# Writing the order of a spectrum filter loop by hand: groups and blocks in a software pipeline, program order pinned on three engines

## The chip, the cores and the metric

The kernel runs on one core of a Trainium2 chip. The metric is the device time of one execution in microseconds (us), the median of the runs named.

The engines are called by their short names: PE is the matrix engine, PEld its weight loads, DVE the vector engine, ACT the scalar engine, POOL (or GpSimd) the general one, SP the sync engine, whose queue issues most transfers.

## The reference

It is the backward pass of a gated sum of two filters over a sequence of 2048 positions and 1024 channels in bf16, together with the forward result:

```
g   = sigmoid((x * gate_w).sum(-1))
a   = irfft2(rfft2(x) * W)              # filter over sequence and channels
b   = causal convolution of B_u with a kernel K made from 12 parameter arrays (FFT of length 4096) + B_u * Dskip
out = g * a + (1 - g) * b
# the outputs: out, and the gradients of 12 inputs for a given grad_out
```

The part at issue is the stage that applies K's spectrum to two signals at once (one of the forward and one of the backward pass). We call it the filter stage. It works through the 1024 channels in eight blocks of 128.

## The kernel before

For each block the filter stage does five things. "First" is a short transform of the input by PE, evacuated by ACT into `st`, which DVE transposes to `Si`. "Second" transforms again, for 17 frequencies in groups of four, four, four, four and one; ACT evacuates to `XG`. "Products" multiplies by the spectrum `kb` on DVE into `PY`. "Inverse" takes `PY` through PE and ACT to `Vt`, and "lags" correlates another part of `PY` on PE. After the five groups DVE transposes `Vt` to `Vr`, and "last" finishes the block in four pieces: PE matmuls, then five DVE instructions with loaded tiles `am`, `gm`, `gom`, and two stores.

```
def middle(bi, Si):
    for gi, (p0, nk_) in enumerate(GRP):                 # (0,4) (4,4) (8,4) (12,4) (16,1)
        # load kb; second: XG  (PE reads Si[:, :, f, :], two bf16 out of every 64)
        # products: m, n -> PY      (DVE)
        # inverse:  PY -> Vt        (PE, ACT)
        # more products: g1, g2 -> PY[..., 256:384]   (DVE)
        # lags: PY -> pq            (PE)
    turn(Vr, Vt)                                         # two DVE transposes, 4.4 us
    return Vr

def last(bi, Vr):
    for hq in range(H16 // HQ):                          # four pieces
        am, gm, gom = three tiles, two buffers each
        nc.sync.dma_start(out=am[:], in_=av3[:, hs, csl])
        nc.sync.dma_start(out=gm[:], in_=gxv3[:, hs, csl])
        nc.sync.dma_start(out=gom[:], in_=gov3[:, hs, csl])
        # 8 matmuls Vr -> py
        TT(out=t_[:], in0=py[:, :, 0, :], in1=omg2[...], op=ALU.mult)
        TT(out=gm[:], in0=py[:, :, 1, :], in1=gm[:], op=ALU.add)
        TT(out=am[:], in0=t_[:], in1=am[:], op=ALU.add)
        TT(out=t_[:], in0=gom[:], in1=am[:], op=ALU.mult)
        nc.vector.tensor_reduce(out=ggall[:, bi, hs], in_=t_[:], axis=AX.X, op=ALU.add)
        nc.sync.dma_start(out=o0v[:, hs, csl], in_=am[:])
        nc.sync.dma_start(out=gxv3[:, hs, csl], in_=gm[:])      # the scratch gm was loaded from

xgs = load_pair(0)
Si = fwd1(0, xgs)                                        # "first" and its transpose
for bi in range(DC):                                     # eight blocks
    Vr = middle(bi, Si)
    if bi + 1 < DC:
        if bi % 2 == 1:
            xgs = load_pair((bi + 1) // 2)
        Si = fwd1(bi + 1, xgs)
    last(bi, Vr)
```

A scheduler may move instructions of one engine against each other where their data allow it, so the order in the program is only where it starts from. After the filter stage comes "the tail", which turns lags into gradients of the parameters; it begins with loads of 1.57 and 1.05 MB of parameters, 1.38 MB of a table `ORJ`, and tiles `A2t`.

## Time and profile before

| | before |
|---|---|
| time, median of the 4 runs beside the changed kernel | 1990.86 us |
| filter stage (first `Si` transpose to the sum that follows the last piece) | 1043.7 to 1752.7 us |
| from `Vr` transpose to `Vr` transpose, seven blocks | 88.2 us mean, 85.3 or 92.1 each but the first |
| tail | 239 us |

First the window table of the kernel before over most of the stage: how long each engine was busy (instructions in brackets), the granted clock of PE as a share of full speed, the mean busy share of the DMA engines, GB/s.

```profile
core 0: us, PE busy (x) PEld busy (x) DVE busy (x) ACT busy (x) POOL busy (x), PEclk, DMA share, GB/s
1045.00:1661.00 616.00, 357.96 (x1832) 210.29 (x1833) 311.83 (x615) 178.27 (x191) 0.00 (x0) 0.74 0.25 50
```

No engine is full: PE 58%, DVE 51%, ACT 29%. The clock of 0.74 belongs to the same picture. The Trainium skill, "TensorE: Matmul & The Clock Gate", Part 1: The HAM clock gate, says that the default is half the clock and that only sustained work lifts it. One 256-column matmul with a contiguous input follows the other by 0.107 us inside busy stretches (granted clock 1.00 at 1105.5 us) and by about 0.213 us after idle ones (granted clock 0.50 at 1231 us, after 13.4 us of idling).

The list of waits of the stage in the kernel before says who waits for whom: engine and what it was to work on, what came last, total us, number of waits, longest.

```profile
DVE m L985 <- ACT XG L922: 231.6, 33, 8.5
PEld L1003 <- DVE PY L988: 134.8, 32, 4.8
DVE gm L1043 <- DMA gm<-gx_scr: 61.0, 7, 13.3
DVE am L1044 <- DMA am<-a_scr: 22.1, 8, 11.7
```

DVE waits for ACT's evacuation of the second stage, PE waits for DVE's products: each group is a chain handed from engine to engine. The last two lines are waits for loads at block ends, 83 us in all. The largest of the `am` waits, 11.7 us, stands at the stage's end. The DVE timeline of one block end in the kernel before shows them (start in us, length, engine, line, instruction, and in brackets the idle time before it with what ended it; `...` marks lines left out):

```profile
1282.79 4.50 DVE L939 STREAM_TRANSPOSE Vr<-Vt 128x2048 f32<-128x2048 f32 x2 [0.42 <-ACT Vt L922]
1291.10 0.69 DVE L1042 TENSOR_TENSOR t__10724<-f_10715,omg_101 128x512 bf16<-128x512 f32 x1 [3.81 <-PE f_10715 L1040]
1292.30 4.49 DVE L939 STREAM_TRANSPOSE Si<-st 128x2048 f32<-128x2048 f32 x2
...
1311.87 0.69 DVE L1043 TENSOR_TENSOR gm<-f_10761,gm 128x512 bf16<-128x512 f32 x1 [11.38 <-DMA gm<-gx_scr]
...
1316.08 0.68 DVE L985 TENSOR_TENSOR m<-XG,kb 128x1024 bf16<-128x1024 bf16 x1
```

From the transpose of `Vr` to the first product of the next block DVE needs 33.3 us, of which 11.4 and 1.3 us are waits for loads, 3.8 us a wait for PE. The rest is DVE's own work: two transposes and most of the four pieces of the last stage.

### The profile page before, as it was taken

What the parts mean: (1) busy time and instruction counts of PE and PEld (TensorE: products, weight loads), DVE (VectorE), ACT (ScalarE), POOL (GpSimd) and SP (SyncE); (2) the same over time, 40 slices, a digit from 0 to 9 for tenths busy, and PEclk for the clock granted to TensorE, in tenths of its full rate; (3) what the DMA queues carried; (4) which work ended last, traced back from release to release, by engine and by line L of the source; (5) the groups of instructions that cost most, each with busy time, mean ns of one, the idle gap of its engine ahead of it and who ended that gap; (6) DMA issues with size and microseconds to landing.
All of it is one profiled execution on the core that took longest, in us unless ns stands there. A gap on an engine that the chain in (4) does not pass through costs nothing.

```text
span 1992.0 us, 25908 instructions
## 1 busy us (share of the span) xinstructions
PE 1206.2 (61%) x10318; PEld 732.4 (37%) x10342; DVE 1223.7 (61%) x2033; ACT 787.2 (40%) x820; POOL 45.3 (2%) x158
## 2 busy tenths in 40 slices
PE   1787668761036495757626465746546565549995
PEld 1444344430013253434413242423323343237773
DVE  8545667529889777876244546445445545537886
ACT  4443234323376957674232222313232332135441
POOL 0000012100000000000010000000000000000000
PEclk9999989995555575757767777868677776757777
DMA  2322523223123223322060512240241202386661
GB/s 88 97 43 85 165 81 81 66 76 98 38 79 131 106 85 124 129 90 101 33 226 12 92 31 64 32 91 15 62 76 47 64 17 64 16 263 215 213 202 43
DMA packets 185887, 181.48 MB, mean 91 GB/s; under 512 B 114723, under 2 KB 148515, under 8 KB 182566
## 3 DMA queue, kind: packets, MB, share of 16 engines
q1 hardware_dynamic: 176806, 175.36, 30.2%
q10 hardware_dynamic: 7632, 3.41, 0.6%
q0 software_dynamic: 1328, 1.05, 0.4%
q8 instruction: 81, 1.33, 0.3%
q14 instruction: 40, 0.33, 0.1%
HBM read 101.29 MB, written 77.95 MB: 90 GB/s over the span
## 4 chain that ended last, share of the span: by engine, by line
PE 42%; DVE 25%; ACT 13%; DMA 12%; issue 6%; SPq 1%; ACTq 0%; POOL 0%; DVEq 0%; POOLq 0%
PE kx L770 5%; PE pq L1019 4%; PE pr L1113 4%; DMA gx_scr<-gm 3%; PE p2i L444 3%; ACT st L922 2%; PE pT L1099 2%; DVE m L985 2%; ACT XG L922 2%; DVE n L986 2%; DMA out_dram<-am 1%; DVE Ue L491 1%; DMA am<-a_scr 1%; ACT Tsb L1103 1%; PE trp L738 1%
## 5 line engine op out<-in xcount | busy, mean ns | idle before, releaser
L985 DVE TENSOR_TENSOR m<-XG,kb 128x1024 bf16<-128x1024 bf16 (+1 forms) x80 | 48.5, 607 | 231.6 <-ACT XG L922 231.6
L1103 ACT ACTIVATE Tsb<-pT 128x672 bf16<-128x672 f32 x128 | 87.3, 728 | 68.6 <-PE pT L1099 67.6
L1099 PE MATMUL pT<-GKq,A2t 32*128 32x42 bf16 x2048 | 84.3, 243 | 43.1 <-DMA A2t<-at_3847 32.7
L1110 DVE TENSOR_TENSOR pd<-Tsb,ORJt 128x5376 bf16<-128x5376 bf16 x32 | 93.8, 2950 | 24.0 <-PE pr L1113 20.6
L1003 PEld LDWEIGHTS <-IC 128*128 128x128 bf16 x120 | 13.1, 127 | 255.6 <-DVE PY L988 134.8
L1019 PE MATMUL pq<-TKT,PY 128*128 128x321 bf16 x544 | 96.5, 333 | 0.0
L1099 PEld LDWEIGHTS <-A2t 32*128 32x128 bf16 x2048 | 65.3, 110 | 66.6 <-issue 63.0
L1113 PE MATMUL pr<-pd,ident 128*128 128x256 bf16 x504 | 77.2, 319 | 4.5 <-DVE pd L1110 4.5
L1019 PEld LDWEIGHTS <-PY 128*128 128x128 bf16 x544 | 59.6, 112 | 32.7 <-DVE PY L1012 1.6
L444 PE MATMUL p2i<-T_131,Z 128*128 128x512 bf16 x224 | 59.1, 381 | 6.8 <-DVE Z L413 3.4
L1113 PEld LDWEIGHTS <-ident 128*128 128x128 bf16 x504 | 54.8, 113 | 22.1 <-issue 6.1
L748 PE MATMUL pK<-wOR,AT 128*32 128x21 bf16 x1024 | 29.7, 207 | 48.0 <-ACT AT L743 24.7
L770 PE MATMUL kx<-Kc,TK_4047 128*128 128x256 bf16 x136 | 41.5, 305 | 22.9 <-DVE spk L778 12.1
L453 DVE CAST UV<-p2i 128x512 bf16<-128x512 f32 x28 | 19.3, 690 | 56.4 <-ACT UV L455 44.7
L743 ACT ACTIVATE AT<-trp 128x1024 bf16<-128x1024 bf16 x32 | 32.6, 1019 | 50.6 <-PE trp L738 50.4
L778 DVE CAST spk<-kx 128x1024 bf16<-128x1024 f32 x16 | 19.6, 1224 | 53.2 <-PE kx L770 53.1
L748 PEld LDWEIGHTS <-AT 128*32 128x32 bf16 x2048 | 23.8, 110 | 77.0 <-ACT AT L743 34.6
L681 PE MATMUL ph<-zrow,Lz 8*128 8x512 bf16 x64 | 30.2, 562 | 29.9 <-ACT EA L682 27.1
L986 DVE TENSOR_TENSOR n<-XG,kb 128x1024 bf16<-128x1024 bf16 (+1 forms) x80 | 48.2, 603 | 0.0
L949 PEld LDWEIGHTS <-S1f 128*128 128x128 bf16 x256 | 25.5, 101 | 59.5 <-issue 53.9
L776 ACT ACTIVATE spk<-kx 128x1024 bf16<-128x1024 f32 (+1 forms) x20 | 18.7, 937 | 66.8 <-PE kx L770 66.8
L939 DVE STREAM_TRANSPOSE Si<-st 128x2048 f32<-128x2048 f32 x16 | 36.0, 2285 | 14.9 <-ACT st L922 14.9
(2555 smaller groups left out, 3620.4 us busy)
## 6 DMA issues: line engine op xcount, KB each, us to landing
tkt_scr<-tst SPq DMA_DIRECT2D x17, 321.0 KB
TKT<-tkt_scr SPq DMA_DIRECT2D x1, 5457.0 KB
Wt<-in_A_w_r_dram SPq DMA_DIRECT2D x32, 128.2 KB
Wt<-in_A_w_i_dram SPq DMA_DIRECT2D x32, 128.2 KB
out_dram<-gw SPq DMA_DIRECT2D x32, 128.2 KB
xt<-in_A_x_dram SPq DMA_DIRECT2D x8, 512.0 KB
xt<-in_grad_out_dram SPq DMA_DIRECT2D x8, 512.0 KB
a_scr<-och SPq DMA_DIRECT2D x16, 256.0 KB
```

What stands on the lines that cost most here:

```text
L444: nc.tensor.matmul(ps[:, ch, :].rearrange("p (w b n) -> p w b n", w=2, b=2), lhsT=Zx[:, comp, ks], rhs=t6(kk, 1 - comp), start=(i_ == 0), ...
L748: nc.tensor.matmul(pK[32 * q:32 * q + 32, c // 16, (c % 16) * NA:(c % 16 + 1) * NA], lhsT=AT[:, comp, cc, 32 * q:32 * q + 32], rhs=wO[:, : ...
L770: nc.tensor.matmul(px[:, k_, comp, :], lhsT=TK[ci][:, k1, comp, :], rhs=Kc[:, ci, :], start=(ci == 0), stop=(ci == 4 and comp == 1))
L922: nc.scalar.activation(out=out, in_=in_, func=ACT.Copy)
L939: nc.vector.transpose(out=d_[:, hf * 2048:(hf + 1) * 2048], in_=s_[:, hf * 2048:(hf + 1) * 2048])
L985: TT(out=m[:, :, c_], in0=xc, in1=kb[:, :, c_, :].unsqueeze(2).to_broadcast([P, nk_, 2, P]), op=ALU.mult)
L986: TT(out=n_[:, :, c_], in0=xc, in1=kb[:, :, 1 - c_, :].unsqueeze(2).to_broadcast([P, nk_, 2, P]), op=ALU.mult)
L1019: nc.tensor.matmul(pq[:, half, 0:NLG // 2], lhsT=PY[:, k_, comp, 256:384], rhs=TKT[:, p0 + k_, comp, half * (NLG // 2):(half + 1) * (NLG / ...
L1099: nc.tensor.matmul(pTs[q // 2][:, q % 2, o_:o_ + 2 * NA], lhsT=A2[32 * q:32 * q + 32, comp, cl * N:(cl + 1) * N], rhs=GKq[32 * q:32 * q + ...
L1103: nc.scalar.activation(out=Tsb[:].rearrange("p m g a (q c) -> p (m g a) q c", q=4)[:, :, qp * 2:qp * 2 + 2, c0_:c0_ + 4], in_=pTs[qp][:, : ...
L1110: TT(out=pd[:], in0=Tsb[:, k_, :, :, :], in1=O_.unsqueeze(1).to_broadcast([P, 2, NA, P]), op=ALU.mult)
L1113: nc.tensor.matmul(pr[:], lhsT=idt[:], rhs=pd[:, :, a_, :], start=(k_ == 0 and a_ == 0), stop=(k_ == 1 and a_ == NA - 1))
```

## The change

Its intent is to keep DVE and PE fed by spreading the work of neighbouring blocks over the groups: the second stage of a group is issued one group ahead, a quarter of the next block's first stage and one piece of the last block's last stage go into each group, lags trail by a group. Every matmul, activation and DVE instruction of the loop is pinned to program order on its engine. The 160 transfers of the last stage go to GpSimd's queue, the loads two pieces ahead, with three buffers; `gm` is stored to a scratch of its own. The diff, cut to its core:

```
+        gx2_scr = dram.tile([S, D], dt.bfloat16, name="gx2_scr")
...
+            def pinned(fn):
+                def run(*a, **k):
+                    return tc.keep_in_program_order(fn(*a, **k))
+                return run
+            TT, MM, AC = pinned(nc.vector.tensor_tensor), pinned(nc.tensor.matmul), pinned(nc.scalar.activation)
+            TR, RD = pinned(nc.vector.transpose), pinned(nc.vector.tensor_reduce)
...  (second, products, inverse, lags, fetch and last become functions of one group or piece; XG gets three buffers)
+                for nm, src in (("am", av3), ("gm", gxv3), ("gom", gov3)):
+                    t_ = fw.tile([P, HQ, P], dt.bfloat16, name=nm, bufs=3)
+                    nc.gpsimd.dma_start(out=t_[:], in_=src[:, hs, csl])
...
+                nc.gpsimd.dma_start(out=gx2v3[:, hs, csl], in_=gm[:])
+                nc.gpsimd.dma_start(out=o0v[:, hs, csl], in_=am[:])
...
             for bi in range(DC):
-                Vr = middle(bi, Si)
-                if bi + 1 < DC:
-                    ...
-                    Si = fwd1(bi + 1, xgs)
-                last(bi, Vr)
...  (the tiles of the block; every second block loads the next pair of inputs)
+                for g in range(NG):
+                    cur = nxt
+                    if g + 1 < NG:
+                        nxt = second(bi, Si, g + 1)
+                    elif more:
+                        nxt = second(bi + 1, Si, 0)
+                    PY = products(g, *cur)
+                    if more and g < 4:
+                        first(bi + 1, xgs, st, 2 * g)
+                    if pend is not None:
+                        lags(bi, *pend, pq)
+                    inverse(g, PY, Vt)
+                    if more and g < 4:
+                        first(bi + 1, xgs, st, 2 * g + 1)
+                    if Vr is not None and g < 4:
+                        last(bi - 1, Vr, g, fts.pop(0))
+                        fts.append(fetch(bi - 1, g + 2) if g < 2 else fetch(bi, g - 2))
+                    if more and g == NG - 2:
+                        Si = new_t("Si")
+                        turn(Si, st)
+                    pend = (g, PY)
+                lags(bi, *pend, pq)
+                Vr = new_t("Vr")
+                turn(Vr, Vt)
+            for g in range(4):
+                last(DC - 1, Vr, g, fts.pop(0))
+                if g < 2:
+                    fts.append(fetch(DC - 1, g + 2))
```

To make room, the tile `gwb` now lives only in the early stage and is loaded again for the tail.

## The prediction

> What bounds the kernel now. The spectrum filter loop runs from about 1045 to 1755 us (timeline), 710 of 1992 us, 86 to 92 us a block. In 1045 to 1661 us (window table) PE is busy 358 of 616 us, DVE 312, ACT 178, DMA 0.25, granted clock 0.74: no engine is full, the loop is a serial chain. By the list of waits DVE waits 232 us for XG (ACT's evacuation of the second stage), PE 135 us for PY in 32 waits and some 120 us more at block ends; DVE waits 83 us more for gm and am loads. The timeline of one group of four frequencies: products 5.9 us on DVE, inverse and lag matmuls, next group's second stage and evacuation, DVE again: 13.7 us. At block ends gm loads wait for gm stores to the same scratch (60.7 us in the sync queue's waits), 17 to 20 us a block.
>
> What the change does. Arithmetic stays. The second stage is issued a group ahead, the first stage of the next block and the last stage of the block before are spread over the groups, lags trail a group, in that order on all three engines. Loads for the last stage are two groups ahead, gm goes to a scratch of its own; the 17 to 20 us leave the chain. Added: 160 natural-layout transfers move from the sync queue to GpSimd's, 20 a block; three GpSimd issues in this trace took 0.56 to 0.90 us, an estimated 11 to 18 us of POOL a block. The Trainium skill, "SBUF - State Buffer", "Who interferes with whom", says DVE's 2-port instructions lock out GpSimd's descriptor writing but two-input tensor_tensor only its reads; this loop has no DVE copies, so I expect no starvation. No run shows it yet.
>
> New group, estimated from traced spacings. PE: 24 matmuls that read Si or Vr with a stride take 0.215 us each, 24 contiguous ones 0.107 warm, 16 lags 0.134 warm: 9.9 us. DVE: products 5.9 plus last stage 2.6. ACT: six evacuations of 1.02. DVE's imaginary part is ready at 3.8, inverse, first and last stage take PE to 8.0, DVE's last stage ends at 10.6: one group 10.6 us, DVE waiting about 2. Block: 4 x 10.6, transpose 4.6, the fifth group's chain 6.3, transpose 4.6: about 58 us. Block one 49, last 49, then 17 for the last four last-stage pieces, six blocks of 58 to 60: about 470 us where 700 stand. I add 20 us for semaphores and a clock below full: the stage ends some 220 us earlier. All is on the critical path: the tail starts when this stage ends.
>
> Predicted 1770 us, 8 in 10 between 1715 and 1830. Faster by over 2%: 0.96, same 0.03, slower 0.01.
>
> Right if: the filter stage takes 470 to 520 us; blocks 56 to 63 us; DVE 75 to 80% and PE over 80% busy there; granted clock above 0.85 (Trainium skill, "TensorE: Matmul & The Clock Gate", Part 1: idling halves the clock; this trace's 0.107 against 0.215 agrees); DVE's waits for XG and gm loads nearly gone, short waits for the last stage's matmuls in their place; tail unchanged at about 237 us.
>
> Wrong if: GpSimd transfers take over 2.5 us each and stall last-stage inputs; three PSUM buffers hold PE behind evacuations more than counted; the granted clock stays at 0.74, making PE the bound at about 12 us a group.

## The result and the profile after

| | before | after |
|---|---|---|
| median of 4 runs each, measured together | 1990.86 us | 1793.08 us |
| filter stage | 709 us | 507 us (1051.7 to 1558.5) |
| a block | 88.2 us | 60.8 to 62.1 us, the six inner ones |
| tail | 239 us | 233 us |

The changed kernel is correct. The ratio is 0.9006 with a 95% interval of 0.8962 to 0.9049. (Every ratio here is the mean time of one kernel's fast runs over that of the kernel before in the same rounds, so it is not quite the ratio of the medians.) The stage became 202 us shorter, and the kernel 198 us.

The window table of the changed kernel over the six inner blocks, with the columns as before:

```profile
1102.00:1472.00 370.00, 270.09 (x1563) 170.59 (x1562) 278.59 (x535) 149.37 (x163) 93.14 (x126) 0.86 0.35 73
```

DVE is now busy 75% of the time, PE 73%, the clock has risen to 0.86, and POOL works 93.14 / 6 = 15.5 us a block on issuing transfers. Part of the gain may be the clock's: for the same matmuls PE is busy 45.0 us a block, where it was 51.1 before (358 us over seven blocks). This was not tested apart from the order. The waits of the changed kernel's stage (every pinned instruction now carries L926, the line of the wrapper, so tiles tell them apart):

```profile
PEld L926 <- DVE Si L926: 59.4, 8, 7.8
PEld L926 <- DVE PY L926: 36.9, 16, 3.7
DVE Vr L926 <- ACT Vt L926: 28.7, 8, 4.7
DVE gm L926 <- DMA gx_scr<-gm: 17.2, 1, 17.2
```

The 231.6 us of waiting for `XG` have gone from this list (the page gives 3.9 us for the corresponding group), and a single long wait for a load is left, at the stage's very end. The profile puts it down to a store of `gm`, but GpSimd's timeline shows the load that DVE needs: it was issued only at 1548.8 us, after GpSimd had waited 10.3 us for a store of `am` to land and free one of the three buffers. What is left of idle time on DVE is seen in its timeline, one group and the end of that block:

```profile
1387.45 1.28 DVE L926 TENSOR_TENSOR m<-XG,kb 128x1024 bf16<-128x1024 bf16 x2
...
1392.96 0.75 DVE L926 TENSOR_TENSOR PY<-m 128x512 bf16<-128x512 bf16 x2
1395.71 0.69 DVE L926 TENSOR_TENSOR t__12149<-f_12140,omg_99 128x512 bf16<-128x512 f32 x1 [2.00 <-PE f_12140 L926]
...
1398.43 4.49 DVE L926 STREAM_TRANSPOSE Si<-st 128x2048 f32<-128x2048 f32 x2
...
1409.74 4.50 DVE L926 STREAM_TRANSPOSE Vr<-Vt 128x2048 f32<-128x2048 f32 x2 [4.26 <-ACT Vt L926]
```

and on PE over the same stretch:

```profile
1389.58 0.28 PE L926 MATMUL f_12114<-PY,IC 128*128 128x256 bf16 x1 [1.35 <-DVE PY L926]
1391.70 0.27 PE L926 MATMUL f_12114<-PY,IS 128*128 128x256 bf16 x1 [1.83 <-DVE PY L926]
1393.77 1.90 PE L926 MATMUL f_12140<-Vr,S1i 128*128 128x256 bf16 x8
1402.98 0.40 PE L926 MATMUL f_12169<-Si,FC 128*128 128x256 bf16 x1 [7.30 <-DVE Si L926]
```

A group takes 10.97 us. PE waits twice for DVE's products, before and in the inverse; only after the inverse does the written order let it do the matmuls of the last stage (`Vr`), and so DVE, done with its products, waits 2.00 us for them. At the block's end DVE transposes `Si` before the products of the fifth group, so PE, whose next matmuls in the written order read `Si`, idles 7.3 us, and DVE then waits 4.26 us for the fifth group's way through PE and ACT. Both engines wait for each other in turn. Whether the data force this or only the written order does, e8 below tells.

### The profile page after: what moved, and what is told of

It is laid out like the page before. It is cut to its first block, busy times and chain, and to the rows that moved or that the text cites. A ratio compares the mean times of both kernels' runs of the same rounds, so it can differ in the third digit from the quotient of the medians.

```text
span 1791.9 us, 25933 instructions
## 1 busy us (share of the span) xinstructions
PE 1162.3 (65%) x10342; PEld 720.7 (40%) x10342; DVE 1236.4 (69%) x2033; ACT 784.9 (44%) x820; POOL 165.2 (9%) x326
## 2 busy tenths in 40 slices
DMA packets 108335, 181.74 MB, mean 101 GB/s; under 512 B 31923, under 2 KB 65715, under 8 KB 105014
## 4 chain that ended last, share of the span: by engine, by line
PE 34%; DVE 27%; issue 16%; ACT 11%; DMA 9%; POOL 1%; SPq 1%; DVEq 0%; ACTq 0%; POOLq 0%
PE kx L771 5%; PE pr L1176 3%; PE p2i L445 3%; DVE m L926 3%; PE pT L1162 2%; DMA gx_scr<-gm 2%; DVE PY L926 2%; DVE Ue L492 2%; ACT Tsb L1166 1%; PE trp L739 1%; DVE junk L344 1%; DVE Si L926 1%; DMA gxc<-gx_scr 1%; DMA tkt_scr<-tst 1%; ACT AT L744 1%
## 5 line engine op out<-in xcount | busy, mean ns | idle before, releaser
L1162 PE MATMUL pT<-GKq,A2t 32*128 32x42 bf16 x2048 | 84.3, 243 | 43.7 <-DMA A2t<-at_3851 33.3
L926 DVE TENSOR_TENSOR m<-XG,kb 128x1024 bf16<-128x1024 bf16 (+1 forms) x160 | 89.8, 602 | 5.5 <-ACT XG L926 3.9
L926 PE MATMUL pq<-TKT,PY 128*128 128x321 bf16 x544 | 86.2, 311 | 0.2 <-DVE PY L926 0.2
L926 DVE TENSOR_TENSOR PY<-m 128x512 bf16<-128x512 bf16 (+1 forms) x240 | 81.3, 379 | 3.5
L926 PEld LDWEIGHTS <-PY 128*128 128x128 bf16 x544 | 55.1, 101 | 24.5 <-DVE PY L926 0.5
L926 PEld LDWEIGHTS <-FC 128*128 128x128 bf16 x256 | 29.5, 115 | 83.6 <-DVE Si L926 59.4
L926 PEld LDWEIGHTS <-IC 128*128 128x128 bf16 x256 | 28.0, 110 | 86.9 <-issue 44.4
L749 PE MATMUL pK<-wOR,AT 128*32 128x21 bf16 x1024 | 29.7, 207 | 48.1 <-ACT AT L744 24.8
L926 DVE STREAM_TRANSPOSE Vr<-Vt 128x2048 f32<-128x2048 f32 x16 | 36.0, 2290 | 28.7 <-ACT Vt L926 28.7
L744 ACT ACTIVATE AT<-trp 128x1024 bf16<-128x1024 bf16 x32 | 32.6, 1019 | 51.1 <-PE trp L739 51.0
L926 DVE STREAM_TRANSPOSE Si<-st 128x2048 f32<-128x2048 f32 x16 | 36.0, 2286 | 24.3 <-ACT st L926 24.3
L682 PE MATMUL ph<-zrow,Lz 8*128 8x512 bf16 x64 | 30.7, 570 | 29.9 <-ACT EA L683 27.0
```

What stands on the lines that cost most here:

```text
L682: nc.tensor.matmul(pz[:, hh * 512:(hh + 1) * 512], lhsT=Lz2, rhs=zrow[:, hh * 512:(hh + 1) * 512], start=True, stop=True)
L744: nc.scalar.activation(out=AT[:], in_=trp[:], func=ACT.Copy)
L749: nc.tensor.matmul(pK[32 * q:32 * q + 32, c // 16, (c % 16) * NA:(c % 16 + 1) * NA], lhsT=AT[:, comp, cc, 32 * q:32 * q + 32], rhs=wO[:, : ...
L926: return tc.keep_in_program_order(fn(*a, **k))
L1162: nc.tensor.matmul(pTs[q // 2][:, q % 2, o_:o_ + 2 * NA], lhsT=A2[32 * q:32 * q + 32, comp, cl * N:(cl + 1) * N], rhs=GKq[32 * q:32 * q + ...
```

## The experiments

Twelve kernels ran. The first four ran on one chip, the other eight on another one, each time beside the kernel before. All but e6 are correct.

### e1, e3: which queue, which scratch

e1 puts the 160 transfers back on the sync queue:

```
-  nc.gpsimd.dma_start(out=t_[:], in_=src[:, hs, csl])      # and the three stores likewise
+  nc.sync.dma_start(out=t_[:], in_=src[:, hs, csl])
```

> The changed kernel with its natural-layout transfers back on the sync queue, nothing else. Theory A (the gain is the hand order and the early loads; the queue that issues them hardly matters): 1785 to 1830 us, blocks 61 to 65 us, same group of 11 us. Theory B (the GpSimd queue is a main part, since stores that wait for DVE would hold up the loads of kb behind them): over 1850 us, with DVE or PE waits for kb or gm in the blocks.

Measured: 1779.37 us, ratio 0.8988 (0.8949 to 0.9027). e3 keeps the queue and stores `gm` to the scratch that it is loaded from, as the kernel before did:

```
-  gx2_scr = dram.tile([S, D], dt.bfloat16, name="gx2_scr")
-  gx2v3 = gx2_scr.rearrange("(r h) d -> r h d", h=H16)
+  gx2v3 = gxv3
```

> The changed kernel with gm stored back to the scratch it is loaded from. Theory A (loads lie two groups ahead, and a load already waits for the landing of a store because of buffer reuse): within 1%, 1780 to 1805 us. Theory C (the scratch of its own is a main part of the gain): over 1830 us, with gm waits back at the blocks.

Measured: 1783.78 us, ratio 0.9020 (0.8979 to 0.9061). Neither differs from the change's 0.9006: in the new order the queue and the second scratch are worth nothing that these runs can see. For the queue this is what the Trainium skill says in "DMA: Bandwidth & Descriptors", Issuing engines are not separate DMA queues: all issuers share the same DMA engines, and another issuer only saves issuing time. Here that saving is not needed; in e1's window of six blocks (368.7 us, against 370.0) POOL is idle and DVE busy 278.62 us, as in the change.

### e4, e5: the transfers alone, in the old order

e4 gives the kernel before the second scratch and nothing else:

```
-  nc.sync.dma_start(out=gxv3[:, hs, csl], in_=gm[:])
+  nc.sync.dma_start(out=gx2v3[:, hs, csl], in_=gm[:])      # and the tail reads gx2v3
```

> The kernel before with the second scratch alone. Theory A (with two buffers each, a gm load still waits for the landing of the store that frees its buffer): 1975 to 1992 us, the 12 us stalls at the block ends stay. Theory C: 1900 to 1940 us, the stalls of 17 to 20 us a block gone.

Measured: 1976.27 us, ratio 0.9987 (0.9944 to 1.0031). e5 gives it the scratch, GpSimd's queue and three buffers for `am`, `gm`, `gom`, all that the change does to transfers apart from their place in the order:

```
+  ... name="am", bufs=3) ... name="gm", bufs=3) ... name="gom", bufs=3)
-  nc.sync.dma_start(out=am[:], in_=av3[:, hs, csl])        # and gm, gom, and both stores
+  nc.gpsimd.dma_start(out=am[:], in_=av3[:, hs, csl])
```

> The kernel before with the whole transfer part of the change (scratch of its own, GpSimd queue, three buffers) and none of the reordering. My split: the block-end stall falls from 17 to 20 us to about 5 us, the groups stay at 13.7 us: 1890 to 1930 us. If the reordering is needed for any gain: 1970 us or more. If the transfers are the whole gain: under 1830 us.

Measured: 1966.64 us beside 1970.37 for the kernel before, ratio 0.9988 (0.9953 to 1.0023). This is a miss: 1890 to 1930 us were expected, and nothing came. The DVE timeline of a block end in e5 shows how little of it the loads held:

```profile
1367.67 4.51 DVE L942 STREAM_TRANSPOSE Vr<-Vt 128x2048 f32<-128x2048 f32 x2 [0.41 <-ACT Vt L925]
...
1390.35 0.69 DVE L1046 TENSOR_TENSOR gm<-f,gm 128x512 bf16<-128x512 f32 x1 [2.50 <-DMA gm<-gx_scr]
...
1394.29 0.43 DVE L1047 TENSOR_TENSOR am<-t__11288,am 128x512 bf16<-128x512 bf16 x1 [2.66 <-DMA am<-a_scr]
1394.63 0.68 DVE L988 TENSOR_TENSOR m<-XG,kb 128x1024 bf16<-128x1024 bf16 x1
```

The waits for loads are down to 5.2 us, yet from the `Vr` transpose to the next block's first product DVE still takes 27.0 us, because the transposes and the four last-stage pieces still stand together there. Against the 33.3 us of the profile before, 6.3 us a block seem saved, but that profile is of another set of rounds, in which the kernel before took some 20 us longer; beside e5 the timed runs show no gain. No profile of the kernel before was kept there, so whether its loads were simply faster is open. What is settled is that the transfers alone give nothing, and that the 10% come from the new order. That order has two parts which no run separates: the order of the engines' work, and the earlier place of the loads. In e5, where the loads kept their place, DVE still waited 59 us for them in the stage, against 83 us in the kernel before and 17 us in the change.

### e2: the written order without the pins

```
-  return tc.keep_in_program_order(fn(*a, **k))
+  return fn(*a, **k)
```

> The changed kernel with the three engines free to be reordered by the scheduler, same program text otherwise. Theory A1 (the text order alone pipelines; pins only tidy): within 2% of the changed kernel, 1770 to 1830 us, blocks 60 to 65 us. Theory A2 (pins are needed): over 1830 us, blocks over 66 us, with PE or DVE waits that the pinned kernel lacks. The compiled order shows PE taking two inverse matmuls ahead and the last stage's before part of the inverse, so I lean to A1.

Measured: 1718.09 us, ratio 0.8676 (0.8637 to 0.8714). This is a miss as well, to the good side. Without the pins the kernel is 3.7% faster than the change (0.8676 / 0.9006 = 0.963): the pins cost time, and the source order in which the work is offered is what helps. The window table of six blocks of e2:

```profile
1088.40:1395.50 307.10, 262.08 (x1565) 167.04 (x1563) 272.39 (x535) 148.65 (x162) 92.52 (x125) 0.90 0.43 88
```

A block is 51.2 us and DVE 89% busy. The timeline shows the scheduler splitting the two halves of the `Si` transpose apart (at 1228.23 and 1233.91 us in one block) with DVE's products between. The wait at the `Vr` transpose that follows is 1.11 us, where the change has 3.6 to 4.3 us.

### e6: does the stride of the second and last stage matter?

The second and last stage read `Si` and `Vr` with a stride of 128 bytes. e6 reads the same number of elements contiguously, which makes the result wrong:

```
-  Ur, Us = Si[:, :, fr, :], Si[:, :, 2 * k1 + 1 if k1 < 16 else 1, :]
+  Ur, Us = Sf[:, fr * 256:(fr + 1) * 256], Sf[:, fs * 256:(fs + 1) * 256]     # Sf: Si flattened; Vr likewise
```

> Wrong result on purpose: the second and last stage read contiguous columns of the same tiles in place of strided ones; all else is the changed kernel. If the stride is what holds these matmuls at 0.215 us, their spacing falls to about 0.107 us when the clock is full, a group from 11.0 to about 10.1 us (eight last-stage matmuls stand on DVE's wait), a block from 61.5 to 56 or 57 us, the kernel to about 1755 us. If it is the clock, the spacing stays 0.215 us and so does the time, 1793 us.

Measured: 1759.11 us (two runs), ratio 0.8929 (0.8887 to 0.8971). PE lines of e6, at a granted clock of 1.00 (1224.0 to 1225.5 us):

```profile
1224.77 0.27 PE L926 MATMUL f<-Si,FC 128*128 128x256 bf16 x1
1224.88 0.27 PE L926 MATMUL f<-Si,FN 128*128 128x256 bf16 x1
1224.99 0.27 PE L926 MATMUL f<-Si,FS 128*128 128x256 bf16 x1
```

They start 0.11 us apart. The strided ones of e8 (below), also at a granted clock of 1.00 (1304.6 to 1308.0 us), start 0.22 us apart:

```profile
1305.28 0.39 PE L926 MATMUL f<-Si,FN 128*128 128x256 bf16 x1
1305.50 0.39 PE L926 MATMUL f<-Si,FS 128*128 128x256 bf16 x1
```

They are no slower where e8's granted clock is 0.51 (1140.0 to 1145.9 us, 0.22 us apart). So it is the stride that costs the factor of two there, not the clock. The Trainium skill, "SBUF — State Buffer", in its note on SBUF cachelines, says that reads which cross to a new 16-byte line pay a penalty; that fits, though it gives no figure for a matmul. The block, however, only falls from 61.6 to 58.0 us, and the kernel by 0.9%, with intervals that overlap. PE's busy time falls by 39 us in the six blocks: 22 us of that make them shorter, and 17 us turn into idling, with the clock down to 0.82. PE's work is thus only part of what bounds the change's loop; what the order of the waits costs, e8 tests.

### e7: the ends of the stage

The last block's wait of 17.2 us for `gm` suggested fetching three pieces ahead with four buffers:

```
-  t_ = fw.tile([P, HQ, P], dt.bfloat16, name=nm, bufs=3)
+  t_ = fw.tile([P, HQ, P], dt.bfloat16, name=nm, bufs=4)      # fetch(n + 3) ahead of last(n); XG: two buffers for three
+  gate = ...                                                   # a GpSimd copy that reads the first XG, ahead of the first fetches; the fetches are pinned too
```

> The changed kernel with the two ends of the stage mended: the first loads of the last stage wait until the first second-stage output is there, loads run three groups ahead with four buffers (the XG buffers go from three to two to make room). If my reading of the two ends is right: first transpose of Si back 8 us earlier, the end after the last Vr transpose from 37 to about 22 us, 1768 to 1780 us. If the ends are bound by something else: within 0.5% of 1793 us.

Measured: 1782.88 us, ratio 0.9047 (0.9022 to 0.9072): no gain. In the trace the stretch from the last `Vr` transpose to the stage's end did fall, from 34.8 to 22.8 us (the expectation's 37 us reach 2 us further, to the tail's first transpose), but the tail grew from 233 to 241 us. The wait of the tail's first matmuls in e7, from the list of waits, and DVE's wait ahead of the tail's first transpose:

```profile
PE pT L1167 <- DMA A2t<-at: 27.9, 1, 27.9
1544.52 1.64 DVE L1151 STREAM_TRANSPOSE GKq<-GKall 128x672 bf16<-128x672 bf16 x2 [7.97 <-DMA out_dram<-am]
```

and the window table of e7 for the 51 us from the last transpose on:

```profile
1512.70:1563.70 51.00, 16.95 (x260) 11.11 (x258) 19.89 (x31) 11.76 (x16) 9.29 (x13) 0.53 0.81 207
```

The sync queue shows the rest: the loads of `ORJ` and of the first `A2t` tile were issued only at 1544.6 and 1544.9 us, 9 us after the stage's end, when the stage's last store of `am` had landed; in the change it was 2.6 us after. The DMA share of 0.81 says what held that store up: from the stage's end to its landing the DMA engines were full, at 393 GB/s (1536.0 to 1544.5 us), with the tail's first loads of 2.6 MB, issued at 1524.4 us, among the transfers. So of the 12.0 us that the stage's end came earlier, 5.4 us were left at the tail's first matmul (39.6 us after the `Vr` transpose, in the change 45.0), and these are 0.3% of the kernel, less than the runs can tell from nothing. Why the tail's loads wait for that store was not tested; presumably their tiles take over its memory.

### e8: another written order, still pinned

This asks whether it is the pins as such, or this order. The matmuls of the last-stage piece and both quarters of the first stage go ahead of the inverse; DVE does the fifth group's products before the `Si` transpose:

```
     PY = products(g, *cur)
     first(bi + 1, xgs, st, 2 * g)
+    first(bi + 1, xgs, st, 2 * g + 1)
     lags(bi, *pend, pq)
+    py = last_mm(Vr, g)
     inverse(g, PY, Vt)
-    first(bi + 1, xgs, st, 2 * g + 1)
-    last(bi - 1, Vr, g, fts.pop(0))
+    last(bi - 1, g, fts.pop(0), py)              # DVE's part only
-    # turn(Si, st) after the fourth group, second(bi + 1, Si, 0) in the fifth
 ...
+    turn(Si, st); nxt = second(bi + 1, Si, 0)    # after the fifth group's lags
     turn(Vr, Vt)
```

> The changed kernel with another order: the last-stage matmuls and both first-stage pieces go ahead of the inverse, and in the fifth group DVE does the products before the Si transpose, PE lags and inverse before the next block's second stage. If DVE's 2.0 us wait a group and 4.3 us a block are the bound that is left: group 10.0 to 10.4 us, block 53 to 56 us, 1740 to 1760 us. If PE is already the bound: the group stays at 11 us, and only the 4 us a block go: 1765 to 1775 us.

Measured: 1689.35 us, ratio 0.8576 (0.8552 to 0.8599), faster than the change, faster than the scheduler's order in e2, and faster than either expectation. Six blocks of e8 in the window table, and DVE's timeline through a block end and one group:

```profile
1091.60:1380.30 288.70, 252.24 (x1560) 161.03 (x1560) 276.54 (x535) 149.13 (x162) 93.23 (x127) 0.93 0.42 93
```

```profile
1167.49 0.75 DVE L926 TENSOR_TENSOR PY<-m 128x512 bf16<-128x512 bf16 x2
1169.24 0.69 DVE L926 TENSOR_TENSOR t__10579<-f,omg 128x512 bf16<-128x512 f32 x1 [0.99 <-PE f L926]
...
1183.45 4.50 DVE L926 STREAM_TRANSPOSE Si<-st 128x2048 f32<-128x2048 f32 x2
1187.87 4.46 DVE L926 STREAM_TRANSPOSE Vr<-Vt 128x2048 f32<-128x2048 f32 x2
```

A block is 48.1 us, DVE is 96% busy, and the transposes follow each other without a gap. A block is 13.5 us shorter than in the change (61.6 in the mean). There DVE had five waits a block, in the block shown three of 2.0, one of 3.1 and one of 4.3 us, and 14.2 us together in the mean of the six blocks. Of these the 1.0 us in the lines above is left: 13.2 of the 13.5 us. DVE's work is nearly the same, 278.59 us in the change's six blocks and 276.54 here. The waits came from the written order.

### e9: the better order without its pins

```
-  return tc.keep_in_program_order(fn(*a, **k))
+  return fn(*a, **k)                              # in e8
```

> The reordered kernel (blocks of 48.1 us, DVE 96% busy, ratio to before 0.8576) without the pins, so that the scheduler may move instructions again. Theory (the pins cost time only where the written order leaves DVE idle; the reordered loop leaves it 4%): within 1.5% of the pinned one, ratio 0.850 to 0.870, blocks 47 to 50 us, DVE 92 to 97% busy. Rival (the scheduler finds better orders than any hand order, as it did in the run without pins): ratio below 0.845. Second rival (the scheduler breaks up the good order, since it splits inverse and second stage and the halves of the transpose): blocks above 50 us, ratio near the 0.868 of the kernel of the change without pins.

Measured: 1725.12 us, ratio 0.8748 (0.8718 to 0.8778). The second rival holds: the scheduler takes the good order apart. Its timeline on DVE:

```profile
1134.82 2.30 DVE L926 STREAM_TRANSPOSE Si<-st 128x2048 f32<-128x2048 f32 x1
...
1143.96 2.30 DVE L926 STREAM_TRANSPOSE Si<-st 128x2048 f32<-128x2048 f32 x1
...
1149.00 4.51 DVE L926 STREAM_TRANSPOSE Vr<-Vt 128x2048 f32<-128x2048 f32 x2 [1.09 <-ACT Vt L926]
```

It again splits the `Si` transpose, now 9.1 us apart, and a block is 52.8 us, with DVE 84% busy. So pins cost 3.7% on the order of the change and win 2.0% (0.8576 / 0.8748 = 0.980) on that of e8. The scheduler comes out at nearly the same block, 51.2 and 52.8 us, whichever of the two orders it starts from.

### e10: both ends together, the tail's loads pinned

```
+  KO = tc.keep_in_program_order                              # in e8, with e7's fetches
-  nc.sync.dma_start(out=parT_[:], ...)                       # at the tail's start; wT, gwb2 likewise
+  if bi == 1: KO(nc.sync.dma_start(out=parT_[:], ...))       # after the first block's A2t tiles
-  nc.sync.dma_start(out=ORJ[:], in_=o_scr[bi][:])            # ahead of the A2t loads
+  if ch == 1: KO(nc.sync.dma_start(out=ORJ[:], in_=o_scr[bi][:]))
-  nc.sync.dma_start(out=A2[:], in_=at_scr[bi][:, ch, :, :])
+  KO(nc.sync.dma_start(out=A2[:], in_=at_scr[bi][:, ch, :, :]))
```

> The reordered kernel with the two ends mended together: fetches a lead of three pieces with four buffers, and the tail's 2.5 MB of parameters and its first ORJ table queued behind the first A2t loads, held there by pins on the sync queue. Theory (the tail's start waits for its own loads: 30.7 us of PE's wait for A2t in the reordered kernel, and the last block's gm wait of 14.8 us): the stage ends 10 to 15 us earlier, PE's wait for the first A2t falls below 10 us, the kernel takes 15 to 30 us less than the reordered one, ratio 0.843 to 0.852. Rival (the tail is bound by the DMA engines' total work, which only moves): ratio 0.855 to 0.860, the tail's length grows by what the stage gained, as in the earlier run that mended the stage's end alone.

Measured: 1775.45 us, ratio 0.9004 (0.8971 to 0.9037), a miss of both theories: 86 us slower than e8. The stage ended 10.7 us earlier, at 1445.3 us, as expected (4.7 us of this because it also began earlier), and the longest wait for `A2t` fell from 30.7 to 18.7 us. But the tail took 329 us instead of 234. The waits of the sync queue in e10 tell why:

```profile
SPq L1231 <- DVE ot L1228: 86.6, 3, 50.4
```

L1231 stores results at the end of each quarter of the tail. In e8 the scheduler issued the next `A2t` loads ahead of those stores, and the same wait there is 6.9 us in all. With the loads pinned they stand behind the stores in the queue, so a load that could have gone waits for DVE's results; DVE then waits up to 22.1 us for PE, PE for `A2t`. From the last `Vr` transpose to the tail's first matmul e10 took 30.4 us, e8 42.3 us, so the tail did start earlier; whether the kernel could keep that, the run does not say. It says that a pin on a shared queue must be judged by what comes to stand in front of it.

### e12: one instruction moved from DVE to ACT

With DVE 96% busy, the scaling in each last-stage piece goes to ACT:

```
-  TT(out=t_[:], in0=py[:, :, 0, :], in1=omg2[:, hs].unsqueeze(2).to_broadcast([P, HQ, P]), op=ALU.mult)
+  for hh in range(HQ):                            # ahead of the inverse
+      AC(out=t_[:, hh, :], in_=py[:, hh, 0, :], func=ACT.Copy, scale=omg2[:, hq * HQ + hh:hq * HQ + hh + 1])
```

> The reordered kernel with one of the five DVE instructions of a last-stage piece (the scaling by one minus the gate, 0.69 us, 0.60 us from start to start) done by four small ACT instructions instead, so 2.4 to 2.8 us a block off DVE and an estimated 5 us a block onto ACT (149 of 288.7 us busy before). Theory (DVE alone bounds the reordered loop): blocks of 45.3 to 46.3 us in place of 48.1, the stage some 16 to 20 us shorter, ratio 0.847 to 0.851. Rival (PE, 252 of 288.7 us busy, and its chain through ACT is nearly as full, so that the freed DVE time becomes a wait): blocks 47.5 us or more, ratio 0.855 or more.

Measured: 1693.72 us, ratio 0.8597 (0.8573 to 0.8622): no gain; the rival holds. Six blocks of e12, then DVE's waits in one of them and PE's timeline of the same group:

```profile
1089.06:1383.05 293.99, 252.56 (x1560) 161.37 (x1561) 262.71 (x512) 173.18 (x258) 93.16 (x127) 0.94 0.42 91
```

```profile
1208.42 0.69 DVE L926 TENSOR_TENSOR gm<-f,gm 128x512 bf16<-128x512 f32 x1 [1.75 <-ACT t__10970 L926]
...
1219.08 0.69 DVE L926 TENSOR_TENSOR gm<-f,gm 128x512 bf16<-128x512 f32 x1 [2.27 <-ACT t__11084 L926]
```

```profile
1198.75 0.37 PE L926 MATMUL f<-Si,FC 128*128 128x256 bf16 x1 [0.41 <-ACT Vt L926]
...
1203.09 2.39 PE L926 MATMUL pq<-TKT,PY 128*128 128x321 bf16 x16
1205.31 1.89 PE L926 MATMUL f<-Vr,S1i 128*128 128x256 bf16 x8
...
1209.35 0.38 PE L926 MATMUL f<-Si,FC 128*128 128x256 bf16 x1 [0.40 <-ACT Vt L926]
```

DVE got 13.8 us lighter in the six blocks, and its waits more than took that up. The PE lines show the reason: from one group's start to the next PE needs 10.6 us with only 0.4 us of idling, while DVE's share of a group is now 8.3 us. DVE's 96% in e8 was an average over two bounds that take turns: PE within the groups, and DVE at the block's end, where it has two transposes to do and PE waits 3.8 us for the first of them.

### e13: the same work, put where PE waits

If that is right, PE's work must leave the groups for the block's end. The lags can:

```
-  if pend is not None:
-      lags(bi, *pend, pq)                         # group g - 1, in every group
+  pys.append(PG)                                  # PG: the lags' input, a tile of its own, four buffers
+  for gl in {3: (0,), 4: (1, 2)}.get(g, ()):
+      lags(bi, gl, pys[gl], pq)
 ...
-  lags(bi, *pend, pq)                             # after the fifth group
+  for gl in (3, 4):
+      lags(bi, gl, pys[gl], pq)
-  XG = fw.tile(..., name="XG", bufs=3)
+  XG = fw.tile(..., name="XG", bufs=2)
```

> The kernel with the scaling on ACT (ratio 0.8597, blocks of 48.8 us, DVE 89% busy, waiting 1.75 and 2.27 us for the second and third last-stage piece of a block), with the lag matmuls taken out of the groups where PE is full and put where PE waits: those of group 0 in group 3, all others at the fifth group, the last two of them under the 3.8 us in which PE waits for the Si transpose. The work is the same; the lag inputs get a tile of their own with four buffers, XG has two buffers in place of three. Theory (inside the groups PE is the bound, 10.6 us from start to start of which 2.1 us are lags, at the block's end DVE is): the two waits fall below 0.8 us each, blocks of 45.5 to 47 us, DVE 92 to 95% busy, ratio 0.845 to 0.854. Rival (the waits come from ACT's queue or from PSUM buffers freed by ACT, not from PE's work): the waits stay at 1.5 us or more, blocks 48 us or more, ratio 0.857 to 0.863.

Measured: 1678.65 us, ratio 0.8486 (0.8454 to 0.8518), as the theory had it, and the fastest kernel. One block of e13 in the window table, and then the only wait that DVE's timeline shows in it:

```profile
1277.50:1322.70 45.20, 41.88 (x260) 27.01 (x260) 43.71 (x86) 28.89 (x43) 15.13 (x22) 0.96 0.40 84
```

```profile
1305.29 0.69 DVE L926 TENSOR_TENSOR gm<-f,gm 128x512 bf16<-128x512 f32 x1 [0.46 <-ACT t__12082 L926]
```

In four of the six blocks the waits stay below 0.9 us and a block takes 45.2 to 45.6 us, DVE 96 to 97% and PE 92 to 93% busy. Two blocks, with waits of 4.0 and 2.8 us for the second piece, miss what was expected and take 49.4 and 49.2 us, so that the mean is 46.6; in them ACT stands up to 6.0 us ahead of an `XG` evacuation, for a reason the records do not show, and PE waits for that. It is not that `XG` has only two buffers: in the first of these blocks DVE had last read the buffer by 1143.4 us, and ACT began to fill it at 1151.3; in the second ACT pauses 3.6 us between the two halves of one buffer. e13 holds e12's move too; the late lags without it were not run. Against the change e13 is 0.8486 / 0.9006 = 0.942, worked out over different rounds and chips.

## Why the prediction was right or wrong

The time was right (1770 predicted, 1793.08 measured, inside 1715 to 1830), and so was its main reason. Point by point:

- **The loop is a chain with no full engine, and reordering shortens it: right.** The whole gain, 198 us, lies in the filter stage (709 to 507 us), and e4 and e5 show that what the change does besides gives nothing alone.
- **"the 17 to 20 us leave the chain": mis-sized, and its share in the gain is not shown.** DVE's waits for loads were 10.2 us a block in the mean (12.7 of 33.3 us at the block end shown), and in the change's inner blocks there are none. But neither the scratch nor the queue did that: the transfers alone (e5) gave 0.9988, and a shared scratch in the new order (e3) 0.9020. What is left is the loads' earlier place in the order. No run separates its worth from that of the engines' order, which spreads over the groups the DVE work that stood together at the block's end.
- **A group of 10.6 us with DVE waiting about 2: nearly right.** It is 10.97, with waits of 2.0 us, one of 3.1 a block, and in every second block one of 4.0. The terms, four groups of 10.6 (measured 45.0 for the four), two transposes of 4.6 (4.4 each) and a chain of 6.3 for the fifth group (6.9), sum to 58; measured 60.8 to 62.1.
- **Edges of the stage: mis-sized.** The last four pieces were given 17 us; from the last `Vr` transpose on, 34.8 us passed, 21.5 with that transpose had been counted. The wait for `gm` of 17.2 us is more than the difference. The terms of the stage summed to 470 us, 37 less than measured; the 20 us added for semaphores and the clock covered half of that, though at least 13 us of it were this wait: so far the nearness of the total is luck. The first transpose of the stage came 8 us later than before. In the experiments it came at 1040.7 to 1042.7 us on the first chip, and on the second at 1047.0 to 1053.0 us, but at 1040.0 and 1045.7 us with e7's gate (e7, e10); the reason was not tested.
- **Tail unchanged at about 237 us: roughly.** It is 233 us, against 239 before: its first loads run under the stage's last waits, and its first matmul comes 10.2 us after the stage's end in place of 14.7. e7 shows that the two trade against each other.
- **PE over 80% busy: wrong,** it was 73%. PE's busy time of 45.0 us a block would be 78% of even the 58 us predicted, so the figure was too high from the start; and the 7.3 us in which PE waits for the `Si` transpose at the block's end are not in the prediction. DVE at 75%, clock 0.86, and POOL at 15.5 us a block (11 to 18 predicted) were right.
- **GpSimd not starved by DVE: right.** The Trainium skill, "SBUF — State Buffer", Who interferes with whom, had been the ground for it. In e8 POOL took 93.23 us for the transfers of six blocks beside a DVE that was busy 96% of the time, the same as the 93.14 us beside the 75% of the change.
- **What the prediction did not ask:** whether the pinned order was a good one. It took "in that order on all three engines" for part of the gain. e2 shows that the pins cost 3.7% there, e8 that another pinned order is 4.8% faster than the change (0.8576 / 0.9006 = 0.952), and e9 that the pins then pay.

## What to carry to other kernels

Where no engine is full, spread the work of neighbouring iterations over the loop first, and then run it with and without pins: a pin is only as good as the order it holds, and a gap that shows up once per iteration as "A waits for B" and again as "B waits for A" is usually an order to mend. A busy share of 96% over a loop does not make an engine the bound of each part of it: moving work off DVE gave nothing until PE's work was moved to the part where PE waits. And before mending a wait at the end of a stage, look at what the next stage waits for.

## What the Trainium skill lacked or had wrong

- "SBUF — State Buffer" (the note on SBUF cachelines): it has no figure for matmul operands. Here 256-column bf16 matmuls that read two elements out of every 64 start 0.22 us apart at granted clocks of 1.00 and of 0.51 (e8), contiguous ones 0.11 us at 1.00 (e6) and about 0.213 us at 0.50 (the kernel before).
- "DMA: Bandwidth & Descriptors" (Issuing engines are not separate DMA queues): its rule held for time (0.8988 on the sync queue, 0.9006 on GpSimd's), but I did not find in it that the records count transfers differently. The same 181.74 MB are 186,032 packets in e1 and 108,335 in the change, by the lines below (first e1, then the change); why was not looked into.

```profile
DMA packets 186032, 181.74 MB, mean 102 GB/s; under 512 B 114740, under 2 KB 148532, under 8 KB 182711
```

```profile
DMA packets 108335, 181.74 MB, mean 101 GB/s; under 512 B 31923, under 2 KB 65715, under 8 KB 105014
```

- No page that I used says that one kernel's time differs by about 1% between sets of rounds. The kernel before had a median of 1991 us beside the change, 1979 us on the first chip of the experiments, and 1970, 1971 and 1978 us in the sets on the second. Whether the chip makes the difference is not shown, but absolute times of different sets should not be compared.
